# A decode block on one core: V loaded in the K cache's layout, w2's first rows ahead of it, and wo's second half in w2's tile

## The chip, the cores and the metric

The kernel runs on one core of one Trainium2 chip. TensorE (PE) does the matrix products, VectorE (DVE) and ScalarE (ACT) the elementwise work, GpSimd (POOL) builds constants, and SyncE (SP) issues nearly all loads; sixteen DMA engines move the data. The metric is the device time of one execution in microseconds (us). Before the change it was 99.94 us, the median of three runs (99.74 to 100.01).

## The reference

One token `x` of 1024 numbers is normalized, and two branches read the result `xn`: attention over the last 4096 positions of a cache with 32 query heads in 4 groups, and a two-layer MLP that normalizes once more. All tensors are bfloat16.

```python
def _A_ref(x, k_cache, v_cache, wq, wo):      # Hq 32, Hkv 4, Dh 128, W 4096
    q = (x @ wq).reshape(B, Sq, Hq, Dh).transpose(0, 2, 1, 3)
    k = jnp.repeat(k_cache[:, :, Sk - W:, :], rep, axis=1)
    v = jnp.repeat(v_cache[:, :, Sk - W:, :], rep, axis=1)
    scores = jnp.einsum("bhqd,bhkd->bhqk", q, k) * (Dh ** -0.5)
    p = _softmax(scores, axis=-1)
    o = jnp.einsum("bhqk,bhkd->bhqd", p, v)
    return o.transpose(0, 2, 1, 3).reshape(B, Sq, Hq * Dh) @ wo

def _B_ref(x, w1, b1, w2, b2):                # w1 1024 x 3584, w2 3584 x 1024
    h = _gelu(jnp.einsum("bsd,df->bsf", _layernorm(x), w1) + b1)
    return jnp.einsum("bsf,fd->bsd", h, w2) + b2

xn = _layernorm(A_x)
return A_x + _A_ref(xn, A_k_cache, A_v_cache, A_wq, A_wo) + _B_ref(xn, B_w1, B_b1, B_w2, B_b2)
```

The weights wq and wo have 8 MiB each, w1 and w2 7 MiB each, and the parts of K and V that are read 4 MiB each. With one token, every number that is loaded is used once.

## The kernel before

The 40 MB pass through four tiles of 32 KB per partition (`slot0` to `slot3`), which are used several times:

- `slot0`: K, then w1's second half (`w11`), then wo rows 0 to 15
- `slot1`: wq's first half, then w1's first half (`w10`), then w2 rows 14 to 27
- `slot2`: wq's second half, then V, then wo rows 16 to 31
- `slot3`: the transposed K (`kt_scr`), then w2 rows 0 to 13 in two loads

A "row" here is 128 rows of the matrix, one on each partition. A load into a slot that is used again waits for the last reader of what was there, so w1's first half waits for the wq products, V for the end of the second wq loop, w2's first half for the copies out of `slot3`, and wo's second half for the V loop. SP issues loads in the order of the program, and one that waits holds up those behind it. wo's second half comes in five cuts (8, 4, 2, 1 and 1 rows), so that the end can follow the landings closely.

The order of each engine's work is written out by hand: the class `Plan` records every operation with what it reads and writes, and `emit` puts them out per engine in the order of the program, with semaphore waits where another engine's or a load's result is needed. No scheduler moves anything.

The stages, with lines of the kernel before:

1. *Head.* POOL makes the constants `spread`, `ident_f`, `selq`, `gmask` (L261-276). PE spreads x over 128 partitions with four products with `spread` (L241), DVE copies it (L287) and works out the two layer norms, with sums over partitions by products with ones (L292-317).
2. *Queries and K.* PE runs two loops over wq (L376) into `acc2`. DVE transposes K in 32x32 blocks (L341), and DVE and ACT copy the blocks into `kT` (L346, L350) so that a head's 128 dimensions lie on the partitions. The queries are cast (L395, L396), transposed by small products with `selq`, and cast into `qm`, whose columns outside a group's own heads are zero (L423).
3. *Scores.* Each quadrant of 32 PE columns takes a quarter of the keys: 32 products of 512 columns into `sc_ps` (L235, `sc_ps<-kT,qm`). One partition row of `sc` thus holds one quarter of the keys for one head.
4. *Softmax.* DVE and ACT copy the scores (L434, L435); the row maximum goes through a transpose and two small steps to `nmx`; ACT takes the exponential into `e128` and its sums into `l_loc` (L457); DVE transposes the exponentials in blocks into `eTb` (L461). The sum over the quarters is a product with `sel4`, its reciprocal is `rs` (L465), and `grs` is `gmask` times `rs` (L467).
5. *MLP.* w1's products run on PE between these steps. DVE adds b1 (`h_pre`, L471), ACT takes the gelu (`h_sb`, L473), DVE transposes it (`hT`, L475) and casts the column to `hTf` (L477). Then DVE does 21 of w2's 28 rows as `run += row * hTf[c]` over 128x1024 numbers, in two accumulators (`running`, L486, L489): nine before the attention output and twelve after it. PE does the other seven (`PE_ROWS`).
6. *V.* V lies with 32 consecutive keys of all four groups on each partition, four pieces of 8192 bytes. 32 products in a loop of two steps (`pe_loop`, `v_step`, L502) take one key per partition, against V's 512 columns, 128 for each of the four groups. Only the columns of a head's own group are wanted: DVE multiplies by `grs` (L518), sums over the groups (L520) and casts (`o_bf`, L522).
7. *Output.* PE spreads `o_bf` over 128 partitions (`o8`), does w2's seven rows and wo's rows 0 to 23 into `sc_ps` (called `bulk` there; `bulk_rows`, L235). DVE adds its accumulators (L525), then the two halves of `bulk` (L557). PE's last eight wo rows and products that sum `run` over the partitions go into `acc2`; two casts (L576, L577) and two stores end it.

The first two loads are issued ahead of the plan, and x alone by ACT:

```python
k_rows = A_k_cache[0, :, Sk - W:Sk, :].rearrange("g (r c) d -> r g (c d)", r=P // Hkv)
```

So K has on partition 4r+g the 128 consecutive keys r of group g, one piece of 32768 bytes.

Of the kernel before, what the change touches and what calls it, by code (L numbers as in the profile page):

```python
# [7 lines left out]
FP32 = mybir.dt.float32  # L8
BF16 = mybir.dt.bfloat16
ACT = mybir.ActivationFunctionType  # L10
ALU = mybir.AluOpType
AX = mybir.AxisListType
# [130 lines left out]
def kernel(  # L143
# [15 lines left out]
    P = 128  # L159
    D = A_x.shape[-1]  # L160
# [4 lines left out]
    Hq = NQ // Dh  # L165
# [18 lines left out]
    def sb(name, shape, dt):  # L184
        return nc.alloc_sbuf_tensor(name, shape, dt).ap()

    def ps(name, shape):
        return nc.alloc_psum_tensor(name, shape, FP32).ap()
# [5 lines left out]
    misc = ps("misc", [P, 512])  # L194
    qo_ps = ps("qo_ps", [P, 512])
# [20 lines left out]
    def op(eng, fn, r=(), w=()):  # L216
        plan.add(eng, fn, r, w)

    def dma(eng, out_ap, in_ap, r=(), w=(), over=()):
        q = plan.engines[eng]  # L220
        plan.add(eng, lambda: q.dma_start(out=out_ap, in_=in_ap), r, w, True, over)  # L221

    def ldw(w_ap, pos, r):
        def go():
            with nc.discard():
                i = pe.ldweights(w_ap, tile_position=pos).ins
            return pe.add_instruction(mybir.InstLdweights(  # L227
                name=nc.get_next_instruction_name(), engine=i.engine, tile_size=(P, 32), tile_position=pos, ins=i.ins, outs=i.outs))
        op("pe", go, r, ())

    def mm(out_ap, w_ap, x_ap, start, stop, pos, r, w):
        def go():
            with nc.discard():
                i = pe.matmul(out_ap, lhsT=w_ap, rhs=x_ap, start=start, stop=stop, tile_position=pos).ins
            return pe.add_instruction(mybir.InstMatmult(  # L235
                name=nc.get_next_instruction_name(), engine=i.engine, start_tensor_calc=start, stop_tensor_calc=stop,
                tile_size=i.tile_size, tile_position=i.tile_position, ins=i.ins, outs=i.outs, ldweights=False))
        op("pe", go, r, w)

    def mm32(out_ap, w_ap, x_ap, start, stop, r, w, pos=None):  # L240
        op("pe", lambda: pe.matmul(out_ap, lhsT=w_ap, rhs=x_ap, start=start, stop=stop, tile_position=pos), r, w)  # L241
# [10 lines left out]
    for i, a, b in wq_cuts:  # L252
# [6 lines left out]

    spread = sb("spread", [Hq, 4, P], BF16)  # L260
# [3 lines left out]
    ident_f = sb("ident_f", [P, P], FP32)  # L264
    op("pool", lambda: pool.memset(ident_f, 0.0), (), ("ident_f",))
    op("pool", lambda: pool.affine_select(out=ident_f, in_=ident_f, compare_op=ALU.not_equal, fill=1.0, base=0,
                                          pattern=[[-1, P]], channel_multiplier=1), ("ident_f",), ("ident_f",))
# [4 lines left out]
    gmask = sb("gmask", [Hq, Hkv], FP32)  # L272
    op("pool", lambda: pool.memset(gmask, 1.0), (), ("gmask",))
    op("pool", lambda: pool.affine_select(out=gmask, in_=gmask, compare_op=ALU.is_ge, fill=0.0, base=0,
                                          pattern=[[-REP, Hkv]], channel_multiplier=1), ("gmask",), ("gmask",))
    op("pool", lambda: pool.affine_select(out=gmask, in_=gmask, compare_op=ALU.is_ge, fill=0.0, base=REP - 1,
                                          pattern=[[REP, Hkv]], channel_multiplier=-1), ("gmask",), ("gmask",))
# [3 lines left out]

    x_ps, tot = misc[:, 0:C], misc[:, 16:17]
    tot2 = misc[:, 32:34]
    for u in range(4):
        mm32(x_ps, spread[:, u, :], x32[:, 8 * u:8 * u + 8], u == 0, u == 3, ("spread", "x32"), ("misc",))
    xf = sb("xf", [P, C], FP32)
    op("dve", lambda: dve.tensor_copy(out=xf, in_=x_ps), ("misc",), ("xf",))  # L287
# [32 lines left out]
    op("dve", lambda: dve.tensor_reduce(out=sel4, in_=ident_f.rearrange("p (r h) -> p h r", r=4), axis=AX.X, op=ALU.add), ("ident_f",), ("sel4",))  # L320
    qm = sb("qm", [P, Hkv, Hq], BF16)
# [11 lines left out]
                                          compare_op=ALU.is_equal, fill=0.0, base=0, pattern=[[-1, Hq], [0, Hq]], channel_multiplier=1), ("xb32",), ("run0",))  # L333

# [45 lines left out]
    qz, zrow = qm.rearrange("p g h -> p (g h)")[0:Hq, :], spread.rearrange("p u n -> p (u n)")  # L380
# [18 lines left out]
    v_sb = slot[2]  # L399
    v4 = v_sb.rearrange("p (g c d) -> p g c d", g=Hkv, c=NCH)  # L400
    dma("sp", v_sb.rearrange("p (g n) -> p g n", g=Hkv), A_v_cache[0, :, Sk - W:Sk, :].rearrange("g (p c) d -> p g (c d)", p=P), (), ("v0",), ("slot2",))

# [18 lines left out]
    qm_d = qm.rearrange("p g h -> p (g h)")  # L421
    qm_d = bass.AP(tensor=qm_d.tensor, offset=qm_d.offset, ap=[list(qm_d.ap[0]), [Hq + REP, Hkv], [1, REP]])
    op("dve", lambda: dve.tensor_copy(out=qm_d, in_=qT_ps.rearrange("p k g -> p g k")), ("qo",), ("qm",))  # L423
    for g in range(Hkv):
        for R in range(4):
            ldw(qm[:, g, :], (0, 32 * R), ("qm",))
        for a in range(2):
            for R in range(4):
                kv = kT[:, R, :, :].rearrange("p u (b r h) -> p h b u r", r=8, h=Hkv)[:, g, 16 * a:16 * a + 16]
                mm(sc_ps[32 * R:32 * R + 32, a, :].rearrange("p (b r u) -> p b u r", r=8, u=4), qm[:, g, :], kv,  # L430
                   g == 0, g == Hkv - 1, (0, 32 * R), kt_keys, (f"sc{a}",))
# [4 lines left out]
    w2_t = [slot[i][:, :14 * D].rearrange("p (r n) -> p r n", r=14) for i in (3, 1)]  # L436
    for a, b in ((0, 6), (6, 14)):
        dma("sp", w2_t[0][:, a:b, :], w2_v[:, a:b, :], (), (f"w20{a}",), kt_srcs)
# [6 lines left out]
    m_row = sb("m_row", [1, Hq], FP32)  # L445
    op("dve", lambda: dve.tensor_reduce(out=m_row, in_=mT_ps.rearrange("a (r h) -> a h r", r=4), axis=AX.X, op=ALU.max), ("misc",), ("m_row",))
    m_rep = sb("m_rep", [1, 4, Hq], FP32)
    op("dve", lambda: dve.tensor_copy(out=m_rep, in_=m_row.unsqueeze(1).to_broadcast([1, 4, Hq])), ("m_row",), ("m_rep",))
    mc_ps = misc[:, 128:129]
    mm32(mc_ps, m_rep.rearrange("a r h -> a (r h)"), ones_f[0:1, 0:1], True, True, ("m_rep", "ones_f"), ("misc",))  # L450
# [8 lines left out]
    eTb = sb("eTb", [P, WQ4 + 96], BF16)  # L459
    op("pool", lambda: pool.memset(eTb[:, WQ4:], 0.0), (), ("eTb_pad",))  # L460
    op("dve", lambda: dve.transpose(out=eTb[:, :WQ4], in_=e128), ("e128",), ("eTb",))  # L461
# [4 lines left out]
    grs = sb("grs", [Hq, Hkv], FP32)  # L466
    op("dve", lambda: dve.tensor_scalar_mul(out=grs, in0=gmask, scalar1=rs), ("gmask", "rs"), ("grs",))  # L467


    h_pre = sb("h_pre", [P, 2, NH], FP32)  # L470
    op("dve", lambda: dve.tensor_tensor(out=h_pre, in0=acc2[:, :, :NH], in1=b1x.rearrange("p (b n) -> p b n", b=2), op=ALU.add), ("acc2", "b1x"), ("h_pre",))  # L471
    h_sb = sb("h_sb", [P, 2 * NH], BF16)
    op("act", lambda: act.activation(out=h_sb, in_=h_pre.rearrange("p b n -> p (b n)"), func=ACT.Gelu_apprx_tanh), ("h_pre",), ("h_sb",))  # L473
    hT = sb("hT", [P, CW2, 32], BF16)
# [4 lines left out]
    def w2_row(c):  # L479
        i, r = divmod(c, 14)  # L480
        return w2_t[i][:, r, :], "w21" if i else f"w20{0 if r < 6 else 6}"
# [11 lines left out]
    for c in dve_rows[:9]:  # L493
        running(c)


    o_all = qo_ps[0:Hq, :]
    v_in = ("eTb", "eTb_pad", "v0", "slot2")

    def v_step(c, first, last):  # L500
        cols = eTb[:, bass.ds(32 * c, P)] if not isinstance(c, int) else eTb[:, 32 * c:32 * c + P]
        return pe.matmul(qo_ps, lhsT=cols, rhs=v4[:, :, c, :], start=first, stop=last)  # L502
# [12 lines left out]
    for a, b in zip(cuts[:-1], cuts[1:]):  # L515
        dma("sp", wo_t[1][:, a:b, :], wo_v[:, 16 + a:16 + b, :], (), (f"wo1{a}",), ("slot2",))
    o_m = sb("o_m", [Hq, Hkv, Dh], FP32)
    op("dve", lambda: dve.tensor_tensor(out=o_m, in0=o_all.rearrange("h (g d) -> h g d", g=Hkv), in1=grs.unsqueeze(2).to_broadcast([Hq, Hkv, Dh]), op=ALU.mult), ("qo", "grs"), ("o_m",))  # L518
    o_f = sb("o_f", [Hq, Dh], FP32)
    op("dve", lambda: dve.tensor_reduce(out=o_f, in_=o_m.rearrange("h g d -> h d g"), axis=AX.X, op=ALU.add), ("o_m",), ("o_f",))  # L520
    o_bf = sb("o_bf", [Hq, Dh], BF16)
    op("dve", lambda: dve.tensor_copy(out=o_bf, in_=o_f), ("o_f",), ("o_bf",))  # L522
    for c in dve_rows[9:]:
        running(c)
# [15 lines left out]
    hcol = lambda c: hT[:, c, 0:1]  # L540
    o8_ps = misc[:, 160:192]
# [5 lines left out]
    bulk_rows(PE_ROWS, w2_row, hcol, "hT", first=True)  # L547

# [5 lines left out]
    bulk_rows(list(range(16)), wo_row, ocol, "o8")  # L554
    bulk_rows(list(range(16, NB)), wo_row, ocol, "o8", last=True, groups=2)
# [57 lines left out]
```

## Time and profile before

| what | value |
|---|---|
| median of the three runs | 99.94 us (99.74 to 100.01) |
| the profiled execution's own time | 99.68 us |
| its span, first to last instruction | 98.4 us |
| DMA read | 39.86 MB, 405 GB/s over the span |
| DVE busy | 73.1 us (74%), 75 instructions |
| PE busy | 56.0 us (57%), 323 instructions |
| ACT, POOL busy | 30.8 us, 9.9 us |
| mean granted PE clock | 0.931 of full speed |

The profile comes from one execution. Its page shows the busy share of each engine in 40 slices of 2.46 us (tenths; 9 is 90% or more), the granted PE clock in the same slices, and the busy share of the sixteen DMA engines. The chain that ended last is followed back from the last instruction through whatever released each step. A line of a timeline has the start in us, the length, the engine, the line of the kernel, the operation, output<-inputs with shapes, a count, and in brackets the engine's idle time before it and who ended it. A line of windows has a stretch, its length, the busy time of PE, weight loads, DVE, ACT and POOL, each with its count, then the granted clock, the DMA share and GB/s. The trace also holds a record of every DMA packet with its start, length and size.

### The profile page before, as it was taken

The numbers are of one execution on the slowest core, as the hardware profiler recorded it, in microseconds if no ns is written. First come the engines' busy times: TensorE is split into PE (matmuls) and PEld (weight loads), VectorE is DVE, ScalarE is ACT, GpSimd is POOL, SyncE is SP. The second block draws the span as 40 slices with busy tenths as digits, with TensorE's granted clock in tenths as the row PEclk, the third lists the DMA queues.
The fourth block names the chain that finished last, engine by engine and source line by source line (L and its number), as shares of the span: only waits on it lengthen the run. The fifth ranks groups of instructions, "written<-read, shape, count | busy, mean of one in ns | idle before, by whom it ended". The sixth has DMA issues, their size and how long they took to land.

```text
span 98.4 us, 951 instructions
## 1 busy us (share of the span) xinstructions
PE 56.0 (57%) x323; PEld 16.0 (16%) x220; DVE 73.1 (74%) x75; ACT 30.8 (31%) x29; POOL 9.9 (10%) x22
## 2 busy tenths in 40 slices
PE   0140400699200699930899547977771839595792
PEld 0040000133000234300212211211210101111130
DVE  0146407999999999999005595999989999999231
ACT  0600000099999899992002193000000000000001
POOL 0626810000000670000000000000000000000000
PEclk9999999999996559999579998599999999999999
DMA  3999979999999899989799999999898999999980
GB/s 60 487 426 453 440 310 470 433 533 426 440 426 403 373 385 513 408 373 513 330 426 426 423 438 430 425 426 480 385 524 343 433 426 433 426 433 406 396 323 1
DMA packets 3084, 39.86 MB, mean 405 GB/s; under 512 B 390, under 2 KB 396, under 8 KB 780
## 3 DMA queue, kind: packets, MB, share of 16 engines
q1 hardware_dynamic: 3034, 39.86, 95.7%
q10 hardware_dynamic: 50, 0.00, 0.0%
HBM read 39.86 MB, written 0.00 MB: 405 GB/s over the span
## 4 chain that ended last, share of the span: by engine, by line
DMA 67%; PE 22%; issue 4%; SPq 2%; DVE 0%
DMA slot<-in_A_wq_dram 29%; DMA slot<-in_A_wo_dram 21%; DMA slot<-in_A_v_cache_dram 17%; PE qo_ps L502 12%; PE acc L376 9%; SPq L221 2%; PE acc L241 1%; DVE res L576 0%; PE acc L235 0%
## 5 line engine op out<-in xcount | busy, mean ns | idle before, releaser
L346 ACT COPY kT<-slot 32x1024 bf16<-32x1024 bf16 (+1 forms) x18 | 23.9, 1327 | 15.9 <-DVE slot L341 15.7
L489 DVE SCALAR_TENSOR_TENSOR run<-slot,hTf,run 128x1024 f32<-128x1024 bf16 x20 | 24.2, 1272 | 0.1
L376 PE MATMUL acc<-slot,xw 128*128 x48 | 15.4, 495 | 13.7 <-DMA slot<-in_A_wq_dram 13.7
L341 DVE STREAM_TRANSPOSE slot<-slot 128x4096 bf16<-128x4096 bf16 x4 | 17.4, 4414 | 3.6 <-DMA slot<-in_A_k_cache_dram 3.6
L502 PE MATMUL qo_ps<-slot,eTb 128*128 (+1 forms) x32 | 11.6, 437 | 4.3 <-issue 2.6
L350 DVE COPY kT<-slot 32x4096 bf16<-32x4096 bf16 x10 | 13.2, 1320 | 0.2
L235 PE MATMUL sc_ps<-slot,o 128*1 128x512 bf16 x48 | 9.1, 378 | 4.3 <-DMA slot<-in_A_wo_dram 4.3
L376 PEld LDWEIGHTS acc<-slot,xw 128*128 x48 | 5.5, 115 | 24.3 <-issue 21.9
L577 ACT CAST res<-acc 33x224 bf16<-33x224 f32 x1 | 0.3, 339 | 20.5 <-PE acc L235 20.5
L235 PE MATMUL sc_ps<-kT,qm 128*32 128x512 bf16 x32 | 5.3, 853 | 0.3 <-DVE qm L423 0.3
L502 PEld LDWEIGHTS qo_ps<-slot,eTb 128*128 (+1 forms) x32 | 3.1, 97 | 12.5 <-issue 9.8
L545 ACT CAST o<-misc 128x32 bf16<-128x32 f32 x1 | 0.2, 186 | 15.0 <-PE misc L241 15.0
L227 PEld LDWEIGHTS <-o 128*1 128x1 bf16 x40 | 2.4, 83 | 13.9 <-issue 13.3
L435 DVE COPY sc<-sc_ps 128x512 f32<-128x512 f32 x1 | 0.7, 691 | 4.9 <-PE sc_ps L235 4.9
L241 PE MATMUL acc<-spread,qm 32*128 32x512 bf16 x4 | 1.6, 498 | 3.7 <-POOL qm L322 3.7
L235 PE MATMUL sc_ps<-slot,hT 128*1 128x512 bf16 x14 | 3.2, 378 | 0.5 <-DMA slot<-in_B_w_dram 0.5
L235 PE MATMUL acc<-slot,yT 128*1 128x448 bf16 x64 | 3.4, 353 | 0.0
L434 ACT COPY sc<-sc_ps 128x512 f32<-128x512 f32 x1 | 0.6, 585 | 8.0 <-PE sc_ps L235 8.0
L241 PE MATMUL qo_ps<-selq,q_sb 128*128 128x4 bf16 x8 | 0.4, 166 | 4.3 <-DVE q_sb L395 4.3
L241 PE MATMUL misc<-x,spread 32*128 32x8 bf16 x4 | 0.3, 168 | 4.4 <-POOL spread L262 4.4
L557 DVE TENSOR_TENSOR run<-sc_ps,run 33x512 f32<-33x512 f32 x2 | 1.3, 678 | 1.8 <-PE sc_ps L235 1.8
L235 PE MATMUL acc<-slot,o 128*1 128x288 bf16 (+1 forms) x32 | 2.2, 272 | 0.7 <-DMA slot<-in_A_wo_dram 0.6
(88 smaller groups left out, 43.6 us busy)
## 6 DMA issues: line engine op xcount, KB each, us to landing
slot<-in_B_w_dram SPq DMA_DIRECT2D x3, 3584.0 KB, 16.7
slot<-in_A_wo_dram SPq DMA_DIRECT2D x3, 2048.0 KB, 23.7
slot<-in_A_k_cache_dram SPq DMA_DIRECT2D x1, 4096.0 KB, 14.0
slot<-in_A_wq_dram SPq DMA_DIRECT2D x1, 4096.0 KB, 28.6
slot<-in_A_v_cache_dram SPq DMA_DIRECT2D x1, 4096.0 KB, 16.8
slot<-in_A_wq_dram SPq DMA_DIRECT2D x2, 1024.0 KB, 9.8
slot<-in_A_wq_dram SPq DMA_DIRECT2D x1, 2048.0 KB, 19.3
slot<-in_B_w_dram SPq DMA_DIRECT2D x1, 2048.0 KB, 21.5
```

The lines of the kernel that those rows point to most:

```text
L221: plan.add(eng, lambda: q.dma_start(out=out_ap, in_=in_ap), r, w, True, over)
L227: return pe.add_instruction(mybir.InstLdweights(name=nc.get_next_instruction_name(), engine=i.engine, tile_size=(P, 32), tile_position=pos ...
L235: return pe.add_instruction(mybir.InstMatmult(name=nc.get_next_instruction_name(), engine=i.engine, start_tensor_calc=start, stop_tensor_c ...
L241: op("pe", lambda: pe.matmul(out_ap, lhsT=w_ap, rhs=x_ap, start=start, stop=stop, tile_position=pos), r, w)
L341: op("dve", lambda s=s: dve.transpose(out=scr[:, s, :], in_=k2[:, s, :]), ("k", "slot0"), (f"scr{s}",))
L346: op("act", lambda s0=s0, s1=s1, R=R, Cd=Cd: act.copy(out=kT[32 * Cd:32 * Cd + 32, R, s0:s1, :].rearrange("p s (c j) -> p (s c) j", j=32), ...
L350: op("dve", lambda R=R, Cd=Cd: dve.tensor_copy(out=kT[32 * Cd:32 * Cd + 32, R, :, :].rearrange("p s (c j) -> p (s c) j", j=32), in_=T3[32 ...
L376: pe.matmul(acc2[:, b, :], lhsT=xw[:, bass.ds(32 * n + 512 * i, P)], rhs=slot[1 + i][:, bass.ds(1024 * n + 512 * b, 512)], start=False, st ...
L435: op("dve", lambda: dve.tensor_copy(out=sc[:, 0:512], in_=sc_ps[:, 0, :]), ("sc0",), ("scs0",))
L489: op("dve", lambda: dve.scalar_tensor_tensor(out=t, in0=wap, scalar=hTf[:, c:c + 1], in1=t, op0=ALU.mult, op1=ALU.add), (key, "hTf", f"run ...
L502: return pe.matmul(qo_ps, lhsT=cols, rhs=v4[:, :, c, :], start=first, stop=last)
L557: op("dve", lambda half=half: dve.tensor_tensor(out=run[0][0:33, 512 * half:512 * half + 512], in0=bulk[:, half, :], in1=run[0][0:33, 512 ...
```

## The change

- *Loads.* w2's rows 0 to 13 go into `slot2`, in one load instead of two, issued in V's old place. V goes into `slot3` after the kT copies, in one load in K's layout: partition 4r+g has 128 consecutive keys of group g. wo's rows 16 to 31 still go into `slot2`, now after DVE's use of w2 rows 0 to 13.
- *Scores.* Each PE quadrant takes one group's heads and the keys of that group (`qm` has four copies of the queries, one for each key of four, placed in different columns); the maximum and its spreading follow the new order.
- *Masked exponentials.* PE permutes the transposed exponentials with `perm` (made by POOL) into `e_ps`; ACT writes them four times into `eM`, each time scaled by a column of `own`, which is 1 on the partitions of one group and 0 on the others. The first of the four stands ahead of the gelu on ACT, three behind it.
- *V.* Each of the 32 products takes four keys by 32 heads against four keys by 128 dimensions; the four diagonal 32x128 blocks are copied out by DVE, summed, and cast by ACT with `rs` as its scale. `grs` and `gmask` are gone.
- *x* is spread by one product with `fours`, masked with `own`, and reduced on DVE.
- *Order.* DVE does sixteen w2 rows ahead of the attention output and five after it. PE does w2's seven rows ahead of `o8`, and all of wo's rows 0 to 23 two at a time.

```diff
+    e_ps = ps("e_ps", [P, NCH * 4, REP])
...
+    fours = sb("fours", [Hq, P], BF16)
+    op("pool", lambda: pool.memset(fours, 1.0), (), ("fours",))
...
-    gmask = sb("gmask", [Hq, Hkv], FP32)
...
-    for u in range(4):
-        mm32(x_ps, spread[:, u, :], x32[:, 8 * u:8 * u + 8], u == 0, u == 3, ("spread", "x32"), ("misc",))
+    own = sb("own", [P, Hkv], FP32)
+    op("dve", lambda: dve.tensor_reduce(out=own, in_=ident_f.rearrange("p (r g) -> p g r", g=Hkv), axis=AX.X, op=ALU.add), ("ident_f",), ("own",))
+    mm32(x_ps, fours, x32, True, True, ("fours", "x32"), ("misc",))
+    xu = sb("xu", [P, 4, C], FP32)
...
-    op("dve", lambda: dve.tensor_copy(out=xf, in_=x_ps), ("misc",), ("xf",))
+    op("dve", lambda: dve.tensor_reduce(out=xf, in_=xu.rearrange("p u c -> p c u"), axis=AX.X, op=ALU.add), ("xu",), ("xf",))
...
-    qm = sb("qm", [P, Hkv, Hq], BF16)
+    qm = sb("qm", [P, Hkv, 4, Hq], BF16)
...
+    perm = sb("perm", [P, P], BF16)
+    op("pool", lambda: pool.tensor_copy(out=perm.rearrange("p (r g) -> p r g", g=Hkv), in_=ident_f.rearrange("p (g r) -> p r g", g=Hkv)), ("ident_f", "run0"), ("perm",))
...
-    v_sb = slot[2]
-    dma("sp", v_sb.rearrange("p (g n) -> p g n", g=Hkv), A_v_cache[0, :, Sk - W:Sk, :].rearrange("g (p c) d -> p g (c d)", p=P), (), ("v0",), ("slot2",))
+    w2_t = [slot[i][:, :14 * D].rearrange("p (r n) -> p r n", r=14) for i in (2, 1)]
+    dma("sp", w2_t[0], w2_v[:, 0:14, :], (), ("w20",), ("slot2",))
+    v_sb = slot[3]
...
-                kv = kT[:, R, :, :].rearrange("p u (b r h) -> p h b u r", r=8, h=Hkv)[:, g, 16 * a:16 * a + 16]
-                mm(sc_ps[32 * R:32 * R + 32, a, :].rearrange("p (b r u) -> p b u r", r=8, u=4), qm[:, g, :], kv,
+                kv = kT.rearrange("p q s (w u r k) -> p k u (s w) q r", u=4, r=8, k=Hkv)[:, g, u, 16 * a:16 * a + 16, :, :]
+                mm(sc_ps[32 * g:32 * g + 32, a, :].rearrange("p (w q r) -> p w q r", q=4, r=8), qm[:, g, u, :], kv,
...
-    for a, b in ((0, 6), (6, 14)):
-        dma("sp", w2_t[0][:, a:b, :], w2_v[:, a:b, :], (), (f"w20{a}",), kt_srcs)
+    dma("sp", v_sb, A_v_cache[0, :, Sk - W:Sk, :].rearrange("g (r c) d -> r g (c d)", r=P // Hkv), (), ("v0",), kt_srcs)
...
+    for b in range(2):
+        mm32(e_ps[:, 64 * b:64 * b + 64, :], perm, eTb[:, 64 * b:64 * b + 64, :], True, True, ("perm", "eTb"), (f"e_ps{b}",))
     rs_ps = misc[0:Hq, 144:145]
     mm32(rs_ps, sel4, l_loc, True, True, ("sel4", "l_loc"), ("misc",))
...
+    def own_heads(g):
+        op("act", lambda: act.activation(out=eM[:, :, REP * g:REP * g + REP], in_=e_ps, func=ACT.Copy, scale=own[:, g:g + 1]),
+           ("e_ps0", "e_ps1", "own"), (f"eM{g}",))
...
+    own_heads(0)
     h_sb = sb("h_sb", [P, 2 * NH], BF16)
...
+    for g in (1, 2, 3):
+        own_heads(g)
...
-    for c in dve_rows[:9]:
+    for c in dve_rows[:16]:
         running(c)
...
-        return pe.matmul(qo_ps, lhsT=cols, rhs=v4[:, :, c, :], start=first, stop=last)
+            cols, keys = eM_w[:, P * w:P * w + P], v_sb[:, 512 * w:512 * w + 512]
...
-        dma("sp", wo_t[1][:, a:b, :], wo_v[:, 16 + a:16 + b, :], (), (f"wo1{a}",), ("slot2",))
-    o_m = sb("o_m", [Hq, Hkv, Dh], FP32)
+        dma("sp", wo_t[1][:, a:b, :], wo_v[:, 16 + a:16 + b, :], (), (f"wo1{a}",), ("w20",))
+    o_u = sb("o_u", [Hq, 4, Dh], FP32)
+    for u in range(4):
+        op("dve", lambda u=u: dve.tensor_copy(out=o_u[:, u, :], in_=qo_ps[32 * u:32 * u + 32, Dh * u:Dh * u + Dh]), ("qo",), (f"o_u{u}",))
...
-    op("dve", lambda: dve.tensor_copy(out=o_bf, in_=o_f), ("o_f",), ("o_bf",))
-    for c in dve_rows[9:]:
+    op("act", lambda: act.activation(out=o_bf, in_=o_f, func=ACT.Copy, scale=rs), ("o_f", "rs"), ("o_bf",))
+    for c in dve_rows[16:]:
...
+    bulk_rows(PE_ROWS, w2_row, hcol, "hT", first=True)
...
-    bulk_rows(PE_ROWS, w2_row, hcol, "hT", first=True)
...
-    bulk_rows(list(range(16)), wo_row, ocol, "o8")
-    bulk_rows(list(range(16, NB)), wo_row, ocol, "o8", last=True, groups=2)
+    bulk_rows(list(range(NB)), wo_row, ocol, "o8", last=True, groups=2)
```

## The prediction

> **What bounds the kernel now.** The page's slices come first, because they show which resource never rests.
>
> ```profile
> DVE  0146407999999999999005595999989999999231
> PEclk9999999999996559999579998599999999999999
> DMA  3999979999999899989799999999898999999980
> ```
>
> The DMA row is full from the second slice to the last but one; VectorE (DVE) rests only briefly once it is under way. The chain that ended last agrees:
>
> ```profile
> DMA 67%; PE 22%; issue 4%; SPq 2%; DVE 0%
> ```
>
> The trace's packet records show how tight this is. Sorted into sixteen lanes, one for each DMA engine, every lane runs without a hole from 2.1-2.9 us to 95.7-96.1 us; in the first lane the loads lie at 31.98-49.16 (w1), 49.17-58.97 (V), 58.98-62.66 and 62.66-67.56 (w2's first half), 67.56-76.06 (its second), then wo. The 22% of PE in the chain is the V loop (59.51-73.67), which the chain crosses because the loads of wo's second half wait for its slot; they are queued at 73.7-75.5 us, while the lanes are busy with earlier work until about 85.8. So that wait costs nothing now. The bound is bytes through sixteen busy lanes.
>
> What comes second is read from the DVE and PE timelines of the tail:
>
> ```profile
> 90.05 1.23 DVE L525 TENSOR_TENSOR run<-run 128x1024 f32<-128x1024 f32 x1
> 93.11 1.28 DVE L557 TENSOR_TENSOR run<-sc_ps,run 33x512 f32<-33x512 f32 x2 [1.83 <-PE sc_ps L235]
> ...
> 91.18 1.89 PE L235 MATMUL sc_ps<-slot,o 128*1 128x512 bf16 x16 [1.28 <-DMA slot<-in_A_wo_dram]
> 93.67 1.03 PE L235 MATMUL acc<-slot,o 128*1 128x288 bf16 x16 [0.60 <-DMA slot<-in_A_wo_dram]
> 94.55 1.03 PE L241 MATMUL acc<-run,ones_f 128*1 128x288 f32 x8
> 95.41 1.25 PE L235 MATMUL acc<-slot,o 128*1 128x288 bf16 x16
> ```
>
> PE's wo rows wait for their landings, and DVE, done with its own rows at 91.28, waits 1.83 us for them. After the two sums PE runs without a stop except for about 0.1 us before the last wo row. Two chains thus end together, and both hang on landings of wo. DVE's slack is those 1.83 us.
>
> **The change part by part.** All sums are against the profiled execution: 99.68 us, span 98.4 and 1.28 around it. It lies 0.26 under the median 99.94 of the three timed runs (99.74 to 100.01); I carry the difference over to the median.
>
> *The loads.* The same bytes move. V goes from 32 packets of 8192 bytes on each lane (9.85 us in the mean over the lanes) to 8 of 32768, the form of the K load (9.69 in the mean): -0.16. W2's first half goes from 8 of 12288 plus 8 of 16384 (3.69 + 4.89 = 8.58) to 8 of 28672, the form of its second half (8.50): -0.08. Bounds: w1's packets of 28672, in a busier stretch, took 8.56 for eight, and K's worst lane 9.74, so the sum lies between -0.1 and -0.26; I take **-0.24**, the rows nearest in time. No load starts later: w2 takes V's place in the queue and waits for the same loop (42.60), V waits for the kT copies (46.09), 21 us of queued work behind the lanes' front. V now lands about 8.5 us later, at 67.7 instead of 59.4.
>
> The Trainium skill (SBUF — State Buffer, "The DMA setup-cost knee") has it that each transfer carries a fixed cost of about 2 us, and so says to merge transfers; by that estimate one load fewer would give about 97.7. The trace disagrees: in the first lane the packets of w2's two loads join at 62.66.
>
> *wo's second half in w2's tile.* Its loads now wait until DVE has used w2 rows 0 to 13, worked out below as 80.9. The first lane reaches that data at 85.8 - 0.24. An issue takes 0.43 us on SP and the first load of all, issued at 0.80, had its first packet at 2.1. 80.9 + 1.3 = 82.2: 3.3 us to spare, cost nothing. If the cover goes, each microsecond past 84.2 is a microsecond of empty lanes. Behind it on SP are only wo's later cuts and the output.
>
> *The head.* One product and two DVE steps replace four products and a copy: a reduction like sel4's 0.73, then two of about 0.16. POOL loses three gmask steps and gains three for `fours`. qm's memset is four times as large (0.20 to at most 0.8); the memset of b1x comes after it, so SP issues b1's load (11.68) up to 0.7 later, with nothing behind it until w1's first load, which waits for its slot until 25.29. All of it ends by 12.7 or so, and its first user after that is K's transpose (15.28) or wq's loop (18.08), both waiting for DMA: nothing.
>
> *perm* replaces the eTb memset on POOL (35.07), beside DVE's kT copies, which gate q. Its size is that of the 128x128 affine_select, 0.30 us. The copy beside POOL's long affine_select took 2.19 us instead of 1.22, so a DVE copy can be held up: bounds 0 and +0.97; I take +0.3.
>
> *Queries and scores.* qm's cast writes 128 columns instead of 32: 0.19 to about 0.3 (m_rep, 128 columns, 0.21): +0.1. The 32 score products keep their number, their size and a read of eight elements four apart; the write into PSUM becomes contiguous. They took 5.29 us; a group of eight at full clock 0.9, where eight w1 products of 448 columns took 0.38. If the strided write was the reason, up to 2.4 us go; if all four groups ran like the slowest (1.71), 1.5 come. I take 0, as the read is of the same kind.
>
> *The exponentials.* This is the path to the MLP's hidden vector:
>
> ```profile
> 58.72 0.12 DVE L465 RECIPROCAL rs<-misc 32x1 f32<-32x1 f32 x1
> 58.87 0.22 DVE L467 TENSOR_SCALAR grs<-gmask,rs 32x4 f32<-32x4 f32 x1
> 59.01 1.07 DVE L471 TENSOR_TENSOR h_pre<-acc,b1x 128x896 f32<-128x896 f32 x1
> 61.09 1.71 DVE L475 STREAM_TRANSPOSE hT<-h_sb 128x896 bf16<-128x896 bf16 x1 [1.02 <-ACT h_sb L473]
> 62.83 0.18 DVE L477 CAST hTf<-hT 128x28 f32<-128x28 bf16 x1
> 63.13 1.28 DVE L489 SCALAR_TENSOR_TENSOR run<-slot,hTf,run 128x1024 f32<-128x1024 bf16 x1
> ```
>
> Two perm products of 512 columns now stand on PE ahead of the sum of l_loc. They can start when eTb's transpose ends, 58.80, and take 0.4 to 0.9 with their loads; the l_loc product takes 0.22. So the reciprocal, which ran at 58.72 because its product was long done, waits until 59.6-60.1, and h_pre stands behind it on DVE. Less grs' 0.14, h_pre starts 0.7 to 1.1 later: +0.9. ACT's first mask (1024 elements; the exp of 1024 took 1.15, two PSUM copies of 512 2 x 0.58) runs 59.6-60.8, ahead of the gelu but done before h_pre; the other three end near 65.6, before V lands. So the rows start 0.3 + 0.1 + 0.9 = **1.3 us later**, at 64.4. Rows 0 to 13 end 16.3 to 16.5 us after (first 1.21, second 0.66, then 1.205 apart): 80.9. W2's second half, landed at 76, holds up nothing.
>
> *V's product.* Still 32 steps in the same loop, 14.2 us: 67.7 to 81.9. DVE reaches the result after 16 rows, at 83.2, so V is covered by 1.3.
>
> ```profile
> 73.70 0.68 DVE L518 TENSOR_TENSOR o_m<-qo_ps,grs 32x512 f32<-32x512 f32 x1 [0.25 <-PE qo_ps L502]
> 74.42 1.00 DVE L520 TENSOR_REDUCE o_f<-o_m 32x128 f32<-32x512 f32 x1
> 75.45 0.21 DVE L522 CAST o_bf<-o_f 32x128 bf16<-32x128 f32 x1
> ```
>
> Between rows this block cost DVE 73.41 to 75.60 = 2.19. Four copies of 128 columns from PSUM (between 0.19 for 32 columns and 0.69 for 512: about 0.27 each, 1.05) and the reduction (1.03) give 2.1: -0.1. The cast goes to ACT (0.2) on the way to o8, ready at about 86.2. PE has done its seven w2 rows by then (81.9 + 3.1). Wo's rows 0 to 15, now two at a time at 0.47 us a pair (the 1.89 for four pairs), end at 90.0, before row 16's landing at 90.94.
>
> *The end.* DVE is free at 91.28 + 1.3 - 0.1 = 92.5. The products that it waits for end at 93.07 - 0.24 = 92.83. **0.3 us of DVE's slack is left**, and both final chains move with DMA: -0.24. 99.68 - 0.24 = 99.44 for the profiled execution, **99.7 on the median**.
>
> **The rivals.**
> 1. *DVE becomes the bound* (slower). Place: the score products, whose read now takes the four quadrants' columns from the same stretch of kT. If each group ran like the slowest of before (1.71), rows start 2.8 late, DVE is free at 94.0 and its sums end at 95.3; PE then needs 0.86 for the run products and 0.9 for four rows, and the cast starts at 97.2 instead of 96.60: **100.5**. Any delay beyond 1.6 in all costs its excess; it makes the kernel slower from 1.9, and by 0.3 from 2.2. For it: the bounds of perm, scores and masks all end there. Against: gains are possible in the scores too. 0.26.
> 2. *PE's clock is low for V.* PE now idles from 60 to 67.7.
>
> ```profile
> 61.00:64.00 3.00, 3.00 (x8) 0.72 (x7) 2.75 (x3) 0.06 (x1) 0.00 (x0) 0.50 0.98 414
> 65.00:73.00 8.00, 5.67 (x18) 1.62 (x17) 8.00 (x8) 0.00 (x0) 0.00 (x0) 1.00 1.04 446
> ```
>
> The granted clock (third number from the right) was 0.50 early in the loop and 1.00 later, and pairs of steps lay 0.92 us apart in both, so the loop is not bound by the clock. Steps of wq's loop were 0.43 apart at 0.50 and 0.22 at 1.00; if eight V steps lost that difference, V would end 1.7 later, at 83.6, DVE would wait 0.4, and 0.1 of the gain would go: **99.8**. 0.05. The Trainium skill (TensorE: Matmul & The Clock Gate, "Part 1: The HAM clock gate") has the array at half rate until some 3.4 us of work; by that rule V's first steps would be slow. The trace's 0.92 at both clocks speaks against it for this loop.
> 3. *Each load has a cost of its own in the lanes*, as large as the first load's 1.3 us from issue to first packet. One load fewer would then give 99.94 - 1.3 - 0.24 = **98.4**. The lanes without a hole speak against it. 0.02.
> 4. *The loads gain nothing*, because another limit sets the rate: 414 to 454 GB/s in five stretches of unlike packets. Then **99.9**. 0.1.
>
> **How the numbers follow.** The forecast has 0.57. A difference of 0.3%, 0.3 us, is about what a measurement of this kernel can tell. The forecast's 99.7 stands 0.06 above that line, and medians of runs that spread over 0.27 put about half of its chance below the line: 0.3 faster, 0.27 same. Rival 3 adds 0.02 faster, 2 and 4 add 0.15 same with a little on either side, 1 nearly all slower: faster 0.33, same 0.41, slower 0.26. The likeliest's own range is 99.45 to 99.95. The whole range reaches from 99.35 (-0.26 and spread) to 100.7 (rival 1 and 0.2 more).
>
> **What would show it.** Right: V's lanes at 9.7 us and w2's at 8.5; no hole before wo's second half; rows starting near 64.4; DVE still idle before the two sums; last landing near 96.0. Wrong: the sums follow DVE's own add without a gap (rival 1), a hole in the lanes near 85.6 (a late DVE), V steps further apart than 0.46 us.

## The result and the profile after

The changed kernel takes 99.50 us (median of 18 runs, 99.37 to 100.40) where the kernel before takes 99.85 (18 runs), which puts the medians 0.35 us apart. The estimated ratio is 0.9971, with a 95% interval of 0.9957 to 0.9985: 0.29 us less, between 0.15 and 0.43. The profiled executions have spans of 98.4 us before and 98.2 after. Their own times (99.68 and 99.75) can't be compared, as the second spent 1.55 us outside its span and the first 1.28.

The slices and the chain on the page of the changed kernel:

```profile
DVE  0255647999999999999206665999999997999431
PEclk9999999999996559999669998555599999999999
DMA  3999989999999999989989999998998999999980
DVE 55%; DMA 30%; PE 6%; ACT 3%; issue 2%; SPq 2%; DVEq 0%
```

The DMA row is as full as before, so the bound is the same. The chain now shows DVE at 55%, where it showed DMA at 67%. It should not be read as a new bound. Near its end the chain of waits has this:

```profile
77.78 1.28 DVE run L498
79.08 0.33 SPq L222
...
80.87 15.17 DMA slot<-in_A_wo_dram
96.08 0.30 PE acc L236 x2
```

wo's last cut was issued at 80.87, behind DVE's rows, and landed 15.17 us later. A cut of 256 KB does not take that long (the last two cuts together took 1.5 us): it stood behind some 14 us of other loads in the queue. The chain follows what released the issue and cannot see that an earlier issue would have changed nothing.

What tells the bound is how long the sixteen lanes spend on each load. From the packet records, by the bytes moved (us for each stage, and when the last packet of data ended):

| | V | w2 rows 0-13 | w2 rows 14-27 | wo rows 0-15 | end |
|---|---|---|---|---|---|
| before | 9.85 | 8.59 | 8.51 | 9.79 | 95.78 |
| after | 9.71 | 8.53 | 8.52 | 9.77 | 95.59 |

The two loads that changed form took 0.20 less, the end came 0.19 earlier, and the span is 0.2 shorter. Both loads of V are single loads, so its 0.14 comes with the longer packets and not with their number of loads. Over all executions on the chip of the next run the mean span was 98.49 before and 98.19 after: 0.30, a tenth more than in this pair. All but the profiled ones left no packet records, so where the tenth lies is not known.

The tail of the changed kernel, from its DVE and PE timelines:

```profile
82.08 1.18 DVE L531 COPY o_u<-qo_ps 32x128 f32<-32x128 f32 x4 [0.64 <-PE qo_ps L514]
83.29 1.02 DVE L533 TENSOR_REDUCE o_f<-o_u 32x128 f32<-32x512 f32 x1
84.24 6.04 DVE L498 SCALAR_TENSOR_TENSOR run<-slot,hTf,run 128x1024 f32<-128x1024 bf16 x5
90.32 1.23 DVE L538 TENSOR_TENSOR run<-run 128x1024 f32<-128x1024 f32 x1
92.93 1.28 DVE L568 TENSOR_TENSOR run<-sc_ps,run 33x512 f32<-33x512 f32 x2 [1.38 <-PE sc_ps L236]
96.41 0.45 DVE L587 CAST res<-acc 33x288 bf16<-33x288 f32 x1 [2.20 <-PE acc L236]
...
85.62 3.61 PE L236 MATMUL sc_ps<-slot,o 128*1 128x512 bf16 x32 [0.28 <-ACT o L559]
91.00 1.89 PE L236 MATMUL sc_ps<-slot,o 128*1 128x512 bf16 x16 [1.76 <-DMA slot<-in_A_wo_dram]
```

The number in brackets is the idle time. DVE still waits 1.38 us for PE ahead of its sums, PE waits 1.76 for wo's row 16, and all that hangs on that landing (91.18 before, 91.00 now; the sums 93.11 and 92.93; the last cast 96.60 and 96.41) moved by 0.18 or 0.19.

### The profile page after: what moved, and what is told of

It is laid out like the page before. It is cut to its first block, busy times and chain, and to the rows that moved or that the text cites. A ratio compares the mean times of both kernels' runs of the same rounds, so it can differ in the third digit from the quotient of the medians.

```text
span 98.2 us, 956 instructions
## 1 busy us (share of the span) xinstructions
PE 50.6 (52%) x321; PEld 15.2 (15%) x219; DVE 75.3 (77%) x78; ACT 35.3 (36%) x34; POOL 10.6 (11%) x22
## 4 chain that ended last, share of the span: by engine, by line
DVE 55%; DMA 30%; PE 6%; ACT 3%; issue 2%; SPq 2%; DVEq 0%
DVE slot L348 18%; DMA slot<-in_A_wo_dram 15%; DVE run L498 15%; DMA slot<-in_A_k_cache_dram 14%; DVE kT L357 14%; PE sc_ps L236 4%; DVE hT L484 2%; SPq L222 2%; DVE eTb L463 1%; ACT e L460 1%; DVE m_loc L445 1%; DVE h_pre L477 1%; ACT h_sb L480 1%; DVE q_sb L402 1%; DVE run L495 1%
## 5 line engine op out<-in xcount | busy, mean ns | idle before, releaser
L514 PE MATMUL qo_ps<-slot,eM 128*128 (+1 forms) x32 | 11.1, 434 | 12.4 <-DMA slot<-in_A_v_cache_dram 9.3
L236 PE MATMUL sc_ps<-slot,o 128*1 128x512 bf16 x48 | 5.5, 378 | 2.0 <-DMA slot<-in_A_wo_dram 1.8
L514 PEld LDWEIGHTS qo_ps<-slot,eM 128*128 (+1 forms) x32 | 3.1, 98 | 20.1 <-issue 18.0
L473 ACT ACTIVATE eM<-e_ps,own 128x1024 bf16<-128x1024 f32 x4 | 4.2, 1107 | 0.5 <-PE e_ps L242 0.5
L236 PE MATMUL sc_ps<-kT,qm 128*32 128x512 bf16 x32 | 3.9, 643 | 0.4 <-DVE qm L428 0.4
L228 PEld LDWEIGHTS <-o 128*1 128x1 bf16 x40 | 1.7, 83 | 8.1 <-issue 7.0
L321 DVE TENSOR_SCALAR yT<-xn,st 128x8 bf16<-128x8 f32 x1 | 2.1, 2137 | 0.7 <-POOL st L319 0.7
```

What stands on the lines that cost most here:

```text
L236: return pe.add_instruction(mybir.InstMatmult(name=nc.get_next_instruction_name(), engine=i.engine, start_tensor_calc=start, stop_tensor_c ...
L321: op("dve", lambda: dve.tensor_scalar(out=yT, in0=xn, scalar1=st12[:, 2:3], scalar2=st12[:, 6:7], op0=ALU.subtract, op1=ALU.mult), ("xn", ...
L473: op("act", lambda: act.activation(out=eM[:, :, REP * g:REP * g + REP], in_=e_ps, func=ACT.Copy, scale=own[:, g:g + 1]), ("e_ps0", "e_ps1" ...
L514: return pe.matmul(qo_ps, lhsT=cols, rhs=keys, start=first, stop=last)
```

## The experiments

The theory: the gain is the length of the packets of V and of w2's first half, and nothing else that can be measured, since all that the engines do stays behind the loads. Its rivals: the gain comes from the new order of the loads or from less work on the engines; each load has a cost of its own; DVE is next to being the bound.

**The changed kernel once more.** No edit.

> The changed kernel once more, beside the variants. Theory (packets): 0.997 of the kernel before, V's lanes 9.7 us, w2's first half 8.5, DVE idle 1.2 to 1.6 us ahead of its two final sums. Rival (the gain comes from the new order or from the engines' work, not from the packets): the same ratio.

It took 99.47 us, 0.9959 of the kernel before (0.9928 to 0.9989). V's stage was 9.71 and w2's 8.51; DVE waited 1.43. It repeats, and it stands beside the old packets, V in small packets and wo's first half in one load, which ran on the same chip.

**The old packets in the new order.**

```diff
-    dma("sp", w2_t[0], w2_v[:, 0:14, :], (), ("w20",), ("slot2",))
+    for lo, hi in ((0, 6), (6, 14)):
+        dma("sp", w2_t[0][:, lo:hi, :], w2_v[:, lo:hi, :], (), (f"w20{lo}",), ("slot2",))
...
-    dma("sp", v_sb, A_v_cache[0, :, Sk - W:Sk, :].rearrange("g (r c) d -> r g (c d)", r=P // Hkv), (), ("v0",), kt_srcs)
+    v_rows_in = A_v_cache[0, :, Sk - W:Sk, :].rearrange("g (r c) d -> r g (c d)", r=P // Hkv)
+    VCUT = 4
+    for j in range(VCUT):
+        lo, hi = 16384 * j // VCUT, 16384 * (j + 1) // VCUT
+        dma("sp", v_sb[:, lo:hi], v_rows_in[:, :, lo:hi], (), (f"v{j}",), kt_srcs)
...
```

The rest of the edit, left out here, makes the users of the data wait for all the loads.

> The changed kernel with the packets of before: V in four loads of 8192 bytes per partition, w2's first half in two loads (12288 and 16384 bytes). Theory (packets): V's lanes 9.85 us, w2's first half 8.58, together 0.24 longer, so 1.000 of the kernel before (99.75 where the changed kernel has 99.5). Rival (order or engines): 0.997, as the changed kernel. If each load had a cost of its own in the lanes, of a microsecond or more, four loads more would give 1.04.

It took 99.91 us, 1.0017 of the kernel before (0.9988 to 1.0047); ten of its twelve spans were 98.4 to 98.7, where the changed kernel had 98.0 to 98.4 on the same chip. V's stage took 9.92 and w2's 8.58, 0.28 more than the 18.22 of the changed kernel, and the data ended at 95.77 instead of 95.58. DVE's wait ahead of its sums was as long as in the changed kernel:

```profile
93.11 1.28 DVE L573 TENSOR_TENSOR run<-sc_ps,run 33x512 f32<-33x512 f32 x2 [1.45 <-PE sc_ps L236]
...
91.18 1.89 PE L236 MATMUL sc_ps<-slot,o 128*1 128x512 bf16 x16 [1.83 <-DMA slot<-in_A_wo_dram]
```

PE took up row 16 at 91.18 and the sums began at 93.11, to the hundredth as before the change, although order, scores, masks and V's product were all new. So the gain goes with the form of the loads. Four loads more cost 0.28 us in all, which ends the rival that each load costs a microsecond or more. Size and number of loads change together here, but the packet records tell them apart: in a lane, V's packets of 8192 bytes started 0.309 us apart in the mean, and 0.318 where a load ended between them. A load's end thus cost a lane about 0.01 us; the rest is the packets' length.

**V in small packets.** The same edit of V with sixteen loads, of 2048 bytes per partition (`VCUT = 16`); w2's first half stays one load.

> The changed kernel with V in sixteen loads of 2048 bytes per partition. Theory (packets): wo's last packets of 2048 bytes took 83 ns, so 128 of them on a lane take 10.65 us instead of 9.7, with 16 completion writes of about 10 ns 10.8: 1.0 to 1.1 us longer, 1.007 to 1.008 of the kernel before. Rival (the size of V's packets is nothing): 0.997. If a load had a cost of its own in the lanes, far more.

V's stage took 11.00 us instead of 9.71: 1.29 more, where 1.0 to 1.1 was expected. Five of six spans were 99.5 to 99.8, 1.3 to 1.6 longer, and one was 101.0. The times were 101.3 to 104.7, median 104.12, far more than the spans explain and than the 1.007 to 1.008 expected. The part of the time outside the span was 1.5 to 1.6 us in two executions and 4.6 to 5.0 in four; the ratio of 1.0199 (1.0113 to 1.0285) is that of the two. The spans follow the packets. As for the rest, the trace holds a packet of 16384 bytes, of a kind that it calls instruction, from 101.33 to 102.41, after the span's end at 99.45. The profiled executions of two runs below that spent 1.9 us or more outside the span hold one too, and the other eight, with at most 1.6, hold none. Whether it makes the time longer is not shown.

**V in packets of 4096 bytes**, eight loads (`VCUT = 8`).

> The changed kernel with V in eight loads of 4096 bytes per partition. Theory (the size of V's packets sets the length of its stage): wo's packets of 4096 took 158 ns, 64 of them on a lane 10.1 us, with eight completion writes 10.2, against 9.7 with one load: the span 0.45 to 0.5 longer, 98.7, and 1.001 to 1.002 of the kernel before. Rival (only packets of 2048 are slow): the span of the changed kernel, 98.2. The sixteen loads of 2048 had executions with 1.5 and executions with 4.6 us outside the span; if the number of loads is behind that, eight may show it too.

V's stage took 10.33 us, 0.62 more than with one load; 0.45 to 0.5 was expected. Its time tells little: it ran on another chip, where the kernel before itself took from 99.6 to 101.7 us, and it came to 1.0067 (1.0017 to 1.0116), above the 1.001 to 1.002 expected. Outside the span it spent 1.3 to 1.9, so eight loads did not bring back the 4.6. V's stage thus took 9.71 at 32768 bytes, 9.85 (one load) and 9.92 (four) at 8192, 10.33 at 4096 and 11.00 at 2048. The mean distance of a lane's packets inside a load, 1.212, 0.308 and 0.309, 0.160 and 0.083 us, gives 9.70, 9.85 and 9.90, 10.27 and 10.63 for its share of V. So the size of the packets makes most of the difference, and the sixteen loads at most 0.4 of their 1.29.

**One DVE addition more, and two.** The edit for two; for one it has `range(1)`.

```diff
+    for _ in range(2):
+        op("dve", lambda: dve.tensor_tensor(out=sc, in0=run[0], in1=run[1], op=ALU.add), ("run0", "run1"), ("scs0", "scs1"))
     op("dve", lambda: dve.tensor_tensor(out=run[0], in0=run[0], in1=run[1], op=ALU.add), ("run0", "run1"), ("run0",))
```

> The changed kernel with one DVE addition of 128x1024 more (its result is used by nobody) right ahead of the sum of the two accumulators. Theory (loads bound, DVE has 1.38 us of slack): the addition takes 1.2 us of the slack, DVE waits about 0.15 for PE, no time: 0.997 of the kernel before. Rival (slack of 0.3, as predicted): 0.9 us more, 1.006.

> Two such additions. Theory (1.38 us of slack): 2.4 - 1.4 = 1.0 us late at the final sums, 0.9 to 1.0 more than the changed kernel, 1.007 of the kernel before, with no idle time of DVE ahead of the sums. Rival (slack of 0.3): 2.1 more, 1.018. Rival (DVE is not a bound at all): 0.997.

With one the kernel took 99.53 us, 0.9968 (0.9948 to 0.9987), the ratio of the changed kernel. With two it took 100.33, 1.0052 (1.0037 to 1.0067). The line of the sums with one and with two:

```profile
92.95 1.28 DVE L570 TENSOR_TENSOR run<-sc_ps,run 33x512 f32<-33x512 f32 x2 [0.28 <-PE sc_ps L236]
```

```profile
92.72 1.22 DVE L540 TENSOR_TENSOR run<-run 128x1024 f32<-128x1024 f32 x1
94.05 1.28 DVE L570 TENSOR_TENSOR run<-sc_ps,run 33x512 f32<-33x512 f32 x2
97.22 0.45 DVE L589 CAST res<-acc 33x288 bf16<-33x288 f32 x1 [1.89 <-PE acc L236]
```

One addition leaves DVE 0.28 us of idle time. With two the wait is gone, the sums start 1.12 late and the last cast 0.81 late, a little less than the 0.9 to 1.0 expected: it follows the start of the sums by 3.17 us instead of 3.48, as its wait for PE is 1.89 instead of 2.20. DVE's slack in the changed kernel is real and it is 1.4 us: a bound close behind the loads, as the prediction had it, but not as close as its 0.3.

**The old write of the scores.** Only the order of the written elements changes, so the attention is over keys that are out of step with V's.

```diff
-                mm(sc_ps[32 * g:32 * g + 32, a, :].rearrange("p (w q r) -> p w q r", q=4, r=8), qm[:, g, u, :], kv,
+                mm(sc_ps[32 * g:32 * g + 32, a, :].rearrange("p (w r q) -> p w q r", q=4, r=8), qm[:, g, u, :], kv,
```

> The changed kernel with the score products written into PSUM with elements four apart, as before the change (the keys then stand in another order than V's, so the attention is that of mixed-up keys). Theory (the contiguous write made the groups faster): at the granted clock of 0.50 a group of eight takes about 1.7 us instead of 0.9, the 32 products 5.2 to 5.4 us instead of 3.9, and DVE's rows start about 1.3 us later, near 64.0; the time stays that of the changed kernel, as DVE's slack covers it. Rival (the new read of kT made them faster): groups of 0.9 and 3.9 us in all.

The weight loads mark the groups of eight products. The timelines of weight loads, of the changed kernel and then of this one:

```profile
48.29 0.14 PEld L228 LDWEIGHTS <-qm 128*32 128x32 bf16 x4 [0.34 <-issue]
49.19 0.14 PEld L228 LDWEIGHTS <-qm 128*32 128x32 bf16 x4 [0.76 <-issue]
50.12 0.16 PEld L228 LDWEIGHTS <-qm 128*32 128x32 bf16 x4 [0.79 <-issue]
```

```profile
48.45 0.22 PEld L228 LDWEIGHTS <-qm 128*32 128x32 bf16 x4 [0.66 <-issue]
50.15 0.22 PEld L228 LDWEIGHTS <-qm 128*32 128x32 bf16 x4 [1.48 <-issue]
51.86 0.22 PEld L228 LDWEIGHTS <-qm 128*32 128x32 bf16 x4 [1.48 <-issue]
```

The granted clock was 0.50 in both from 48.5 to 50.1. A group takes 0.90 to 0.93 us with the contiguous write and 1.70 to 1.71 with elements four apart; all 32 take 3.91 and 5.90. The read of kT is the same in the two, so it is the write.

At full clock no difference between the two writes is left. In the kernel before, which also writes four apart, the clock went back to 1.00 at 50.64, and the group from 51.19 to 52.10 took 0.91:

```profile
49.95 0.22 PEld L227 LDWEIGHTS <-qm 128*32 128x32 bf16 x4 [1.49 <-issue]
51.19 0.14 PEld L227 LDWEIGHTS <-qm 128*32 128x32 bf16 x4 [1.02 <-issue]
52.10 0.13 PEld L227 LDWEIGHTS <-yT 128*1 128x1 bf16 x4 [0.78 <-issue]
```

And the contiguous form does not follow the clock. In the changed kernel's second run the clock was 1.00 from 50.17 on, and the group from 50.10 to 51.03 took 0.93. With one DVE addition more the clock was 0.50 until 52.15, and yet the line of the products is the same in both runs:

```profile
47.78 3.92 PE L236 MATMUL sc_ps<-kT,qm 128*32 128x512 bf16 x32 [0.39 <-DVE qm L428]
```

So the write cost time only because PE stood at half clock here. What holds a group at 0.9 us otherwise was not tested; the read of eight elements four apart is in both forms.

DVE then starts its rows at 64.58 instead of 62.75 and waits only this long at the end:

```profile
92.91 1.28 DVE L568 TENSOR_TENSOR run<-sc_ps,run 33x512 f32<-33x512 f32 x2 [0.26 <-PE sc_ps L236]
```

The span was 98.2, as in the changed kernel: 1.8 us more ahead of the rows are covered, and 0.26 of cover is left. (There is one execution; its time was 100.16, with 1.96 us outside the span.)

**w2's first half in one load, in the kernel before.**

```diff
-    for a, b in ((0, 6), (6, 14)):
-        dma("sp", w2_t[0][:, a:b, :], w2_v[:, a:b, :], (), (f"w20{a}",), kt_srcs)
+    dma("sp", w2_t[0], w2_v[:, 0:14, :], (), ("w20",), kt_srcs)
...
```

> The kernel before with w2's first half in one load, behind V as it was. Theory of packets alone: 0.08 us less, 0.999. Theory with the covers: the whole half lands near 67.6 instead of its first six rows at 63.1, DVE's rows start 4.5 us later, its wait for V goes and its 1.83 us at the end are used up; it is free near 95.5, and the kernel takes 1.5 to 2.5 us more, 1.015 to 1.025.

It took 103.36 us (four executions, 102.4 to 104.9); the ratio, without the slowest, is 1.0331 (1.0239 to 1.0423), more than the 1.015 to 1.025 expected. In its profiled execution of 102.82 us the stage of w2's first half shrank to 8.51, just as in the changed kernel, and yet:

```profile
64.02 0.18 DVE L476 CAST hTf<-hT 128x28 f32<-128x28 bf16 x1
68.00 1.28 DVE L488 SCALAR_TENSOR_TENSOR run<-slot,hTf,run 128x1024 f32<-128x1024 bf16 x1 [3.80 <-DMA slot<-in_B_w_dram]
...
94.58 1.23 DVE L524 TENSOR_TENSOR run<-run 128x1024 f32<-128x1024 f32 x1
95.91 1.28 DVE L556 TENSOR_TENSOR run<-sc_ps,run 33x512 f32<-33x512 f32 x2
99.08 0.45 DVE L575 CAST res<-acc 33x288 bf16<-33x288 f32 x1 [1.89 <-PE acc L235]
```

DVE waits 3.80 us for the landing and has no wait left at the end; the cast comes 2.48 late, as expected (1.5 to 2.5). So the joined load is free only because w2 now goes ahead of V: the new order gains nothing by itself (the old packets in the new order took 1.0017), but pays for the joining. The time missed the forecast all the same: the profiled execution spent 1.92 us outside its span, two other spans were 102.5 and 102.6, and why its executions lie so far apart was not settled.

**wo's first half in one load, too.**

```diff
-    for a in (0, 8):
-        dma("sp", wo_t[0][:, a:a + 8, :], wo_v[:, a:a + 8, :], (), (f"wo0{a}",), ("slot0",))
+    dma("sp", wo_t[0], wo_v[:, 0:16, :], (), ("wo00",), ("slot0",))
...
```

> The changed kernel with wo's rows 0 to 15 in one load of 32768 bytes per partition instead of two of 16384. Theory (packets): sixteen packets of 16384 took 9.79 us on a lane, eight of 32768 take 9.69, so 0.1 us less than the changed kernel, 0.996 of the kernel before. PE starts on wo's rows at about 86.0 instead of 85.6, when the whole load has landed, and ends row 15 near 89.8, ahead of row 16's landing near 90.8. Rival (a later start of PE's wo rows costs): no gain over the changed kernel or a loss.

It took 99.43 us, 0.9955 (0.9931 to 0.9978). The stage of wo's first half took 9.71 instead of 9.79, the data ended at 95.52 instead of 95.58, and the span was 98.1. PE's new wait is covered:

```profile
86.01 3.62 PE L236 MATMUL sc_ps<-slot,o 128*1 128x512 bf16 x32 [0.65 <-DMA slot<-in_A_wo_dram]
90.91 1.89 PE L236 MATMUL sc_ps<-slot,o 128*1 128x512 bf16 x16 [1.29 <-DMA slot<-in_A_wo_dram]
```

It is faster than the kernel before. Against the changed kernel the lanes show less than a tenth of a microsecond, which the times (99.43 and 99.47) don't tell apart.

## Why the prediction was right, point by point

- *The forecast:* 99.7 from a median of 99.94; measured were 99.50 from 99.85, inside the likeliest range of 99.45 to 99.95. Of the 0.2 between the forecast and the result, 0.09 is the median before, which came out lower in 18 runs than in three.
- *The loads* (-0.24, bounds -0.1 and -0.26): V gave 0.14 and w2 0.06 in the profiled pair, 0.22 together against the repeated run, and taking the old packets back took the gain back. The measured -0.29 (-0.43 to -0.15) holds the term, just inside the 0.3 us called no change.
- *No load starts later:* no hole is in the lanes. V landed for PE at 67.91, forecast 67.7. V was issued at 46.34 and its data moved from 57.30 on, so 11 us of other work stood ahead of it, not the 21 of the working; that is still enough.
- *The packet times* of the working are some 0.3 us late against the profile's zero: the first load's first packet starts at 1.82 instead of 2.1. No length of a stage changes by it.
- *wo's second half:* issued from 79.08, forecast 80.9, and its data moved from 85.30. About 5 us to spare, even after the 1.3 that the working took for an issue: nothing.
- *The head:* DVE was done by 13.4, forecast 12.7, still ahead of K's transpose. Nothing, as said.
- *perm* (+0.3): the ten DVE copies took 13.45 instead of 13.32 us. POOL's copy took 1.27, but only 0.1 of it reached DVE; K's later landing (15.41 instead of 15.28) gave another 0.13.
- *Queries* (+0.1): the cast took 0.29 instead of 0.19.
- *Scores* (0, bounds -2.4 and +1.5): **the term that was mis-sized.** They took 3.91 us instead of 5.29, -1.4. The working took 0 "as the read is of the same kind", but the slow groups of before were slow by the write at half clock: four apart, a group took 1.71 at 0.50 and 0.91 at 1.00, and contiguous 0.9 at both. The -2.4, by which the groups would also have fallen below 0.9 towards the pace of w1's products, did not come either.
- *Exponentials* (+0.9): the reciprocal waited 0.85 for its product; from the end of eTb's transpose to h_pre it was 0.93 instead of 0.21, so +0.7, the lower end. The mask took 1.11.
- *The sum of these:* the rows were forecast 1.3 later, at 64.4, and came 0.4 earlier, at 62.75, all by the scores. With the scores' write put back they came at 64.58 and DVE's last wait was 0.26, forecast 0.3. So the forecast of the time did not hang on the scores. That the two agree so closely is in part luck: the scores took 5.90 there, 0.6 more than before the change, as the clock stayed at 0.50 until 52.24 instead of 50.64, and the other terms together came some 0.5 short.
- *V's product:* still 0.92 us a pair, and it ended at 82.05, forecast 81.9. DVE, being early, now waited 0.64 for it, which gave back part of what the scores had gained: 1.38 of slack instead of the 1.83 of before. The block took 2.16 between rows, forecast 2.1.
- *Rival 1* (DVE): not reached; the two additions show that it is there from 1.4 us on. *Rival 2* (clock): the windows of the V loop, third number from the right the granted clock:

```profile
67.90:70.90 3.00, 3.00 (x7) 0.70 (x7) 3.00 (x4) 0.00 (x0) 0.00 (x0) 0.50 1.05 449
72.00:81.00 9.00, 6.28 (x20) 1.82 (x20) 9.00 (x8) 0.00 (x0) 0.00 (x0) 1.00 1.00 430
```

  PE's clock fell to 0.50 at 60.86, while it stood idle, and V's loop began at half clock and had it until 71.10, for 3.2 us. That agrees with the Trainium skill (TensorE: Matmul & The Clock Gate, "Part 1: The HAM clock gate"), by which idle time brings the array to half rate and some 3.4 us of work bring it back. Before the change the loop began at 1.00 and had 0.50 from 60.88 to 64.29, about as long. About 7 steps in 3 us and 20 in 9 are the same pace, so this loop lost nothing by it. *Rival 3*, and with it the 97.7 of the working, fell with the old packets in more loads, and *rival 4* with the same run, where the gain went away (its five stretches had 409 to 454 GB/s, not 414 to 454).

## What to carry to other kernels

Where every DMA engine is busy from end to end, as here, a change is worth what it takes off the lanes, and that is read from the lengths of packets, not from the chain of waits or from engines' busy time; here 0.2 of 94 us was left in it, most of it in pieces of 8 KB. A load can be joined only where nobody needs its first part early, so the order of the loads may have to change first, and the next bound behind them (DVE, 1.4 us) has to be known to see whether the change in order is free. A stage that speeds up while the time stands still buys slack, and slack can be measured by adding work until the time moves.

## What the runs showed of the hardware

- Products on 32 columns of PE each, four quadrants side by side, ran at half pace when they wrote PSUM with elements four apart and the granted clock was 0.50: 1.70 us for eight products of 512 columns, against 0.90 to 0.93 with the elements next to each other and the same read. At a granted clock of 1.00 a group took 0.91 with elements four apart and 0.93 with them next to each other.
- V's 4 MB took 9.71 us in packets of 32768 bytes, 9.85 to 9.92 in 8192, 10.33 in 4096 and 11.00 in 2048; the end of a load between two packets of 8192 cost a lane about 0.01 us.
- With V in sixteen loads, four of six executions spent 4.6 to 5.0 us outside the span from the first to the last instruction, where the other kernels mostly spent 1.2 to 1.6 and at most 2.4. With eight it did not show. In the traces a packet of kind instruction after the span goes with such a longer rest (three of the eleven profiled executions); the cause is open.
